# Batch 2's second MLP product as three quads of half-size products

## The chip, the core and the metric

The kernel runs on one core of a Trainium2 chip. Five engines work side by side, each through its own instruction stream in program order: TensorE (PE) for matrix products, with weight loads shown beside it as PEld; VectorE (DVE), ScalarE (ACT) and GpSimd (POOL) for elementwise work; SyncE (SP), which here only issues DMAs. The metric is the device time of one execution in microseconds (us), the lower the better. Before the change it is 298.46 us, the median of three runs from 298.05 to 299.08.

## The reference

Inputs are fp32: q, k, v of shape (4, 8, 768, 64), block numbers, and the weights of an MLP. Per batch, cut to what matters:

```python
scores = np.matmul(q, k.T) / 8.0            # 8 heads, 768 x 768
scores = np.where(mask, scores, -1e9)       # blocks of 32, sampled
x = softmax(scores) @ v                     # heads joined: (768, 512)
a1 = alpha1 * x + beta1
u = x + lam * (w_tok @ a1)                  # token product, 768 x 768
a2 = alpha2 * u + beta2
h = np.maximum(a2 @ w_ch1, 0.0)             # first MLP product, 512 -> 2048
out = u + lam * (h @ w_ch2)                 # second MLP product, 2048 -> 512
```

## The kernel before

A batch has 768 tokens, held as 6 tiles of 128, and 8 heads, done as 4 pairs; there are 16 pairs in all, and pairs 12 to 15 are batch 3's. The attention of batch b + 1 is woven with the MLP of batch b. Everything is issued in an order that is written out by hand: tables of strings (`W1`, `W2`, `W2L`, `W3`), each string a row, each letter a job. A letter whose list of jobs is empty does nothing. Every job issues its instructions to all engines at its place, so a letter's place sets its place in the queues of PE, DVE, ACT, POOL and SP at once.

The letters that matter: `q` computes three units of scores on PE and the first exponential on ACT; `x` does the next exponential; `k` multiplies an exponentiated unit by the mask on DVE (line 636); `p` multiplies weights with v on PE, and when a head is complete DVE divides by the sum (lines 688 and 689, a "finish") and the normalised, scaled values `a1pp` are written by POOL, or by DVE for the last pair (lines 705 and 706); `T` is one third of a token product for two pairs (line 846 on PE, then the sum into `x_sb` at line 858 and two casts at 865 on DVE, or the casts on ACT for the last two pairs); `f` is one step of the first MLP product (four products of 384 columns at line 919 on PE, a rectification at line 926 on ACT into `hts`); `g` is one step of the second MLP product; `S` a sum of parts of `hts` on DVE (line 1144); `W` and `A` sums of weights on DVE; `d` a DMA transpose issued by SP; `a` the DVE `a1pp` of the last pair's first head.

Rows of `W2L` are named r0 to r11 here, from the first. Three rows make a pair of heads. The trace shows the scores of r9 at 225.17, of r10 at 229.66 and of r11 at 235.51 us; r5 to r8 begin at 196.74, 203.54, 211.41 and 218.35. After r11 comes the first row of `W3`, which begins `a p p p g s g g T`: the last masks and products with v, the last finish, and the first `T` of the last head pairs.

The hidden values of a batch are in two tiles `hts`: columns c = 0 for token tiles 0 to 2, c = 1 for 3 to 5. `f` fills c = 0 first. A batch's second MLP product is done in one of two ways. Directly (`job_f2`): a token tile takes 4 steps `g` of four products of 512 columns, all into one bank of PSUM, and one DVE add of 512 columns into `x_sb` (line 1067). Or as a quad (`job_p`): two token tiles together are a 2 x 2 block product, which is done with seven products of blocks instead of eight (1 to 7). Each is one step `g` of eight products of 256 columns (line 1170). Beside them stand four DVE sums for the tile pair (`SOP`; 1 and 2 make X1 and X2, 3 and 4 overwrite parts of `hts`) and seven DVE adds into `x_sb` (line 1180), six of 256 columns and one (product 5) of 512. Products 1, 6 and 5 accumulate in one bank, with a DVE add after each; so do 7 and 4. In batch 2, tiles 0 and 3 are done directly and (1, 4) and (2, 5) as quads; batch 3 is three quads.

PSUM tiles `mm` come from a pool of three banks; `f`, `T`, the first unit of a row's scores (two tiles) and most `g` use it. `sp` has two, `op` (the products with v) one.

Of the kernel before, what the change touches and what calls it, by code (L numbers as in the profile page):

```python
# [18 lines left out]
B = 4  # L19
H = 8  # L20
S = 768
# [4 lines left out]
DM = 512  # L26
P = 128
NT = S // P
# [52 lines left out]
]  # L81
W3 = [
# [6 lines left out]
HN = NH // 2  # L89
# [159 lines left out]
def kernel(  # L249
# [16 lines left out]
    nc = tc.nc  # L266
# [194 lines left out]
    def sp_tile():  # L461
        return psum.tile([P, 2, 512], FP, name="sp", tag="sp", bufs=2)
# [6 lines left out]
    def mm_tile(shape=(P, DM), dt=FP):  # L469
        return psum.tile(list(shape), dt, name="mm", tag="mm", bufs=3)  # L470

    def op_tile(shape):
        phase["op"] += 1
        if phase["first"] and phase["op"] % 2 == 0:
            return mm_tile(shape)
        return psum.tile(shape, FP, name="op", tag="op", bufs=1)
# [97 lines left out]
    x_sbs = {}  # L574
# [234 lines left out]
    did = set()  # L809
# [3 lines left out]
    hts = {}  # L813
# [256 lines left out]
    def emit_store(b, o, sl, eng=nc.sync):  # L1070
        eng.dma_start(
            out[b].rearrange("(p o) n -> p o n", o=NT)[:, o, sl], x_sbs[b][:, o, sl]
        )
# [13 lines left out]
    def b_rows(name, n, k=1):  # L1087
        if name in bq:
            rows, cols = bq[name]
            return w2b[:, rows.start + n : rows.start + n + k, cols]  # L1090
        m = HN * ("T1", "T2", "T4", "T3").index(name) + n
        assert m // 6 == (m + k - 1) // 6
        return tpool[m // 6][:, m % 6 : m % 6 + k]
# [21 lines left out]
    def a_of(b, t, name, r=slice(0, HN)):  # L1115
        if name in ("X1", "X2"):
            return xs[(b, t, name)][:, r]
        c, half = {"11": (0, 0), "12": (0, 1), "21": (1, 0), "22": (1, 1)}[name]
        return hts[(b, c)][:, HN * half + r.start : HN * half + r.stop, ts(t, P)]

    SOP = {
        1: ("X1", "21", "22", ALU.add),
# [5 lines left out]
    def job_s(b, t, n, r=slice(0, HN)):  # L1128
        dst, a, c, op = SOP[n]
        rows = range(r.start, r.stop)  # L1130
        for name in (a, c):
            if name[0] == "X":
                assert all(("S", b, t, int(name[1]), m) in did for m in rows)
            else:
                h, half = divmod(int(name) - 11, 10)
                assert all(("f", b, h, HN * half + m) in did for m in rows)
        if n == 3:
            assert all(("S", b, t, 1, m) in did for m in rows)
        if n == 4:
            assert (b, t, 2) in did  # L1140
        if dst[0] == "X" and (b, t, dst) not in xs:
            tag, bufs = ("eT", 6) if b == B - 1 else ("xs", 4)
            xs[(b, t, dst)] = ap_.tile([P, HN, P], BF, name="xs", tag=tag, bufs=bufs)
        nc.vector.tensor_tensor(
            out=a_of(b, t, dst, r), in0=a_of(b, t, a, r), in1=a_of(b, t, c, r), op=op
        )
        did.update(("S", b, t, n, m) for m in rows)
# [8 lines left out]
        7: ("21", "T3", 3),  # L1156
    }
    banks = {}

    def mul(b, t, n, ps, start, cols=slice(0, HC)):  # L1160
        a, m, need = PROD[n]
        assert m in bq or all((m, r) in did for r in range(0, HN, 2))
        if need:
            assert all(("S", b, t, need, r) in did for r in range(HN))
        c, half = {"1": (0, 0), "X": (1, 0)}.get(a[0], (1, 0))
        if need == 0:
            h, half = divmod(int(a) - 11, 10)
            assert all(("f", b, h, HN * half + r) in did for r in range(HN))
        for r in range(HN):
            nc.tensor.matmul(  # L1170
                ps,
                a_of(b, t, a)[:, r],
                b_rows(m, r)[:, 0, cols],
                start=(start and r == 0),
                stop=(r == HN - 1),
                skip_group_check=True,
            )

    def plus(x, ps):
        nc.vector.tensor_tensor(out=x, in0=x, in1=ps, op=ALU.add)  # L1180

    def twice(ps):
        return ps.unsqueeze(1).broadcast_to([P, 2, HC])

    lo, hi = slice(0, HC), slice(HC, DM)

    def job_p(b, t, n):
        x = x_sbs[b]
        last = (b, t) == (B - 1, NT // 2 - 1)
        bk = banks.setdefault((b, t), {})  # L1190
        if n in (1, 2, 7):
            bk[n] = sp_tile()[:, 0] if n == 1 else mm_tile()[:]
        if n == 3 and not last and 2 not in bk:
            bk[2] = mm_tile()[:]
        if n == 1:
            mul(b, t, 1, bk[1][:, lo], True)
            plus(x[:, t, lo], bk[1][:, lo])
        elif n == 2:
            mul(b, t, 2, bk[2][:, lo], True)
            if last or b < B - 1:  # L1200
                plus(x[:, t, lo], bk.pop(2)[:, lo])
            if last:
                emit_store(b, t, lo)
        elif n == 6:
            mul(b, t, 6, bk[1][:, lo], False)
            plus(x[:, t + 3, lo], bk[1][:, lo])
        elif n == 7:
            mul(b, t, 7, bk[7][:, lo], True)
            plus(x[:, t + 3, hi], bk[7][:, lo])
        elif n == 5:  # L1210
            mul(b, t, 5, bk[1][:, lo], False)
            plus(x[:, t : t + 4 : 3, hi], twice(bk[1][:, lo]))
        elif n == 4:
            mul(b, t, 4, bk[7][:, lo], False)
            plus(x[:, t + 3, lo], bk[7][:, lo])
            emit_store(b, t + 3, slice(0, DM))
        elif last:
            for h in range(2):
                sl = slice(HC + h * P, HC + h * P + P)
                ps = (mm_tile(), op_tile([P, DM]))[h]  # L1220
                mul(b, t, 3, ps[:, sl], True, ts(h, P))
                plus(x[:, t, sl], ps[:, sl])
                emit_store(b, t, sl, (nc.sync, nc.scalar)[h])
        else:
            sl = hi if b < B - 1 else slice(0, DM)
            mul(b, t, 3, bk[2][:, hi], b < B - 1)
            plus(x[:, t, sl], bk[2][:, sl])
            emit_store(b, t, slice(0, DM))
        did.add((b, t, n))

    NPAIR = B * NP
# [34 lines left out]
    def start_mlp(b):  # L1266
        if b == B - 1:
            todo["f"] += [
                lambda j=j: job_m(*j) if len(j) == 2 else job_f1(*j) for j in last_f1()
            ]  # L1270
        else:
            todo["f"] += [
                lambda c=c, n=n: job_f1(b, c, n) for c in range(2) for n in range(NH)
            ]
        if b not in STR:
            todo["g"] += [
                lambda o=o, g=g: job_f2(b, o, g) for o in range(NT) for g in range(4)
            ]
            return
        todo["g"] += [  # L1280
            lambda j=j: job_p(b, *j) if len(j) == 2 else job_f2(b, *j[:2])
            for j in P_ORDER[b]
        ]
        todo["S"] += [lambda t=t, n=n, r=r: job_s(b, t, n, r) for t, n, r in S_ORDER[b]]

    REST = (6, 7, 5, 4, 3)
    P_ORDER = {
        2: [(0, g, "g") for g in range(4)]
        + [(t, 2) for t in (1, 2)]
        + [(3, g, "g") for g in range(4)]  # L1290
        + [(t, 1) for t in (1, 2)]
        + [(t, n) for t in (1, 2) for n in REST],
        3: [(t, n) for t in range(2) for n in (1, 2)]
        + [(t, n) for t in range(2) for n in REST]
        + [(2, n) for n in (1, 2) + REST],
    }
    ALL, R1, R2 = slice(0, HN), slice(0, HN // 2), slice(HN // 2, HN)
    S_ORDER = {
        2: [(t, n, ALL) for t in (1, 2) for n in (1, 2, 3, 4)],
        3: [(t, n, R1) for n in (1, 2, 3) for t in range(3)]  # L1300
        + [(t, n, r) for t in range(3) for n, r in ((1, R2), (2, R2), (3, R2), (4, ALL))],
    }

    def start_pair(i):
# [227 lines left out]
```

## Time and profile before

| | |
|---|---|
| median of three runs | 298.46 us (298.05 to 299.08) |
| profiled execution | 298.76 us |
| its span, first to last instruction | 297.1 us |
| granted TensorE clock | 1.0 |
| PE busy | 289.7 us, 98% |
| DVE busy | 237.8 us, 80% |
| ACT busy | 217.1 us, 73% |
| POOL busy | 109.8 us, 37% |

A row of the time line gives the start and the length in us, the engine, the source line, the operation, the tiles written and read, their shapes and how many instructions were merged. The square bracket at its end is the time for which the engine stood idle before it and what ended that. Instructions overlap at their ends, so what one costs in a queue is read from start to start, not from its length. Records of a few matrix products are missing from a trace now and then.

### The profile page before, as it was taken

The page shows a single profiled execution, that of the slowest core. Times are in us where ns is not written, and L with a number is a line of the kernel's source. Part 1 is how long each engine was busy: PE and PEld are TensorE (multiplying, and loading weights), DVE is VectorE, ACT ScalarE, POOL GpSimd, SP SyncE. Part 2 cuts the span into 40 slices and gives each one's busy share as a digit, 9 for nine tenths or more (in the row PEclk, how much of TensorE's full clock was granted, in tenths as well). Part 3 has the DMA queues.
Part 4 walks back from the last instruction along what each step waited for, and adds up shares of the span by engine and source line. Part 5 has one row for each costly group of instructions (what it writes and reads, how often), then busy time and mean ns, then how long its engine had stood idle before and what let it go on. Part 6 is the DMA issues. An engine that isn't in the chain of part 4 may idle for free.

```text
span 297.1 us, 7554 instructions
## 1 busy us (share of the span) xinstructions
PE 289.7 (98%) x3082; PEld 193.5 (65%) x3101; DVE 237.8 (80%) x485; ACT 217.1 (73%) x324; POOL 109.8 (37%) x149
## 2 busy tenths in 40 slices
PE   8999999999999999999999999999999999999995
PEld 3688888665567565565576466556576679665884
DVE  4988899995678796977878777895956899799774
ACT  4999999998899963999779581999869744576000
POOL 8997978632443710355323340335320300000000
PEclk9999999999999999999999999999999999999999
DMA  6999999992392995729955767745520211400032
GB/s 182 184 199 186 192 171 187 171 123 44 95 147 55 112 203 84 118 65 119 125 96 73 124 110 146 103 92 69 70 62 17 38 38 29 141 1 3 0 141 73
DMA packets 57274, 31.09 MB, mean 105 GB/s; under 512 B 37204, under 2 KB 54016, under 8 KB 57240
## 3 DMA queue, kind: packets, MB, share of 16 engines
q0 software_dynamic: 16752, 14.22, 34.4%
q1 hardware_dynamic: 40020, 15.92, 29.3%
q8 instruction: 24, 0.39, 0.6%
q10 hardware_dynamic: 468, 0.47, 0.5%
q14 instruction: 10, 0.08, 0.1%
HBM read 29.75 MB, written 6.29 MB: 121 GB/s over the span
## 4 chain that ended last, share of the span: by engine, by line
PE 84%; DVE 6%; DMA 4%; ACT 3%; issue 1%; POOL 1%; SPq 0%; POOLq 0%
PE mm L919 18%; PE mm L1058 13%; PE sp L601 10%; PE mm L846 8%; PE op L671 7%; PE mm L1170 5%; PE sp L1170 4%; PE mm L601 3%; DVE eT L636 3%; PE mm L822 3%; PE op L648 2%; DMA vr<-in_v_dram 2%; ACT eT L619 2%; PE mm L1016 2%; PE sp L1016 2%; DMA uraw<-ubf 2%
## 5 line engine op out<-in xcount | busy, mean ns | idle before, releaser
L619 ACT ACTIVATE eT<-sp,expb 128x1024 f16<-128x1024 f32 x111 | 118.4, 1120 | 2.1 <-PE sp L601 1.4
L636 DVE TENSOR_TENSOR eT<-eT,mask 128x1024 f16<-128x1024 f16 x99 | 80.6, 843 | 13.5 <-ACT eT L619 13.3
L919 PE MATMUL mm<-uT,w1b 128*128 128x384 bf16 x416 | 76.8, 326 | 0.4 <-ACT hts L926 0.3
L705 POOL TENSOR_TENSOR a1pp<-x_sb,vbc 128x384 bf16<-128x384 f32 x25 | 28.5, 1138 | 119.0 <-DVE x_sb L689 84.7
L619 ACT ACTIVATE eT<-mm,expb 128x512 f16<-128x512 f32 x66 | 41.7, 685 | 26.5 <-PE mm L601 26.3
L926 ACT ACTIVATE hts<-mm 128x384 bf16<-128x384 f32 x104 | 49.1, 502 | 13.3 <-PE mm L919 12.4
L919 PEld LDWEIGHTS <-w1b 128*128 128x128 bf16 x416 | 38.7, 98 | 26.4 <-issue 2.9
L1058 PE MATMUL mm<-w2b,hts 128*128 128x512 bf16 x205 | 52.2, 379 | 0.9 <-issue 0.2
L671 PEld LDWEIGHTS <-eT 128*128 128x128 f16 x792 | 29.8, 98 | 8.8 <-issue 1.7
L1058 PEld LDWEIGHTS <-hts 128*128 128x128 bf16 x224 | 19.8, 98 | 22.3 <-issue 3.9
L671 PE MATMUL op<-vext,eT 128*128 128x65 f16 x792 | 32.1, 194 | 0.4 <-DVE x_sb L689 0.3
L601 PE MATMUL sp<-qTs,kTs 88*128 88x512 bf16 (+1 forms) x120 | 26.9, 325 | 1.2 <-ACT eT L619 0.7
L706 POOL TENSOR_TENSOR a1pp<-a1pp,vbc 128x384 bf16<-128x384 bf16 x25 | 26.7, 1069 | 2.0
L846 PE MATMUL mm<-a1pp,wtokT 128*128 128x256 bf16 x216 | 25.9, 273 | 0.1
L846 PEld LDWEIGHTS <-wtokT 128*128 128x128 bf16 x216 | 20.6, 98 | 5.6 <-issue 1.8
L1170 PEld LDWEIGHTS <-hts 128*128 128x128 bf16 x208 | 19.5, 98 | 3.0 <-issue 0.3
L858 DVE TENSOR_TENSOR x_sb<-x_sb,mm 128x512 f32<-128x512 f32 x18 | 12.3, 686 | 9.9 <-PE mm L846 9.8
L601 PE MATMUL sp<-qhT,khT 64*128 64x256 bf16 (+1 forms) x176 | 19.8, 322 | 0.0
L601 PEld LDWEIGHTS <-khT 64*128 64x128 bf16 x264 | 10.6, 94 | 12.7 <-issue 9.2
L648 PEld LDWEIGHTS <-eT 128*128 128x128 f16 x360 | 14.9, 97 | 3.8 <-issue 0.3
L689 DVE TENSOR_TENSOR x_sb<-op,rcp 128x384 f32<-128x384 f32 x28 | 15.6, 558 | 1.0
L1067 DVE TENSOR_TENSOR x_sb<-x_sb,mm 128x512 f32<-128x512 f32 x14 | 9.6, 686 | 8.2 <-PE mm L1058 6.7
(135 smaller groups left out, 376.9 us busy)
## 6 DMA issues: line engine op xcount, KB each, us to landing
out_dram<-x_sb SPq DMA_DIRECT2D x23, 256.0 KB
qpad<-in_q_dram POOLq DMA_DIRECT2D x15, 192.0 KB, 4.6
kr<-in_k_dram POOLq DMA_DIRECT2D x15, 192.0 KB, 5.3
vr<-in_v_dram POOLq DMA_DIRECT2D x15, 192.0 KB, 6.3
w1b<-in_moe_w_ch_dram POOLq DMA_DIRECT2D x4, 512.0 KB, 9.2
w2b<-in_moe_w_ch_dram POOLq DMA_DIRECT2D x4, 512.0 KB, 7.7
hts<-in_moe_w_tok_dram POOLq DMA_DIRECT2D x2, 576.0 KB, 8.7
x_sb<-in_k_dram ACTq DMA_DIRECT2D x2, 192.0 KB
```

The source lines that it names most:

```text
L601: nc.tensor.matmul(sp[jj][:, dst], lhsT, rhs, start=True, stop=True, skip_group_check=True,)
L619: nc.scalar.activation(dst, at, AF.Exp, bias=expb[:], scale=SCALE)
L636: nc.vector.tensor_mul(out=e, in0=e, in1=keep)
L648: nc.tensor.matmul(op[0][:, o, :], ets[u][:, jj, h * QB + n * P : h * QB + n * P + P], vexts[i % NVB][:, w, 2 * jp + jj, :], start=op[1] == 0,
L671: nc.tensor.matmul(op[0][:, o, :], ets[u][:, jj, h * QB + n * P : h * QB + n * P + P], vexts[i % NVB][:, w, 2 * jp + jj, :], start=op[1] == 0,
L705: eng.tensor_tensor(out=dst, in0=x_sbs[b][:, :, cols], in1=bc[0], op=ALU.mult)
L706: eng.tensor_tensor(out=dst, in0=dst, in1=bc[1], op=ALU.add)
L846: nc.tensor.matmul(ps[:, o], wtokT[:, os_, ts(2 * n + o, P)], a1pps[i][:, os_, :], start=(os_ == 0 and o == 0), stop=(os_ == NT - 1 and o ...
L919: nc.tensor.matmul(ps[:, 0:QC], w1b[:, dk, ts(n, P)], uTs[b][:, dk, ts(c, QC)], start=(dk == 0), stop=(dk == 3),)
L926: nc.scalar.activation(h_row(b, c, n), ps[:, 0:QC], AF.Relu)
L1058: nc.tensor.matmul(ps[:], ht[:, nk, ts(o % 3, P)], w2b[:, nk, :], start=(nk == 0), stop=(nk == NH - 1),)
L1170: nc.tensor.matmul(ps, a_of(b, t, a)[:, r], b_rows(m, r)[:, 0, cols], start=(start and r == 0), stop=(r == HN - 1), skip_group_check=True,)
```

## The change

Batch 2's second MLP product becomes three quads: tiles (0, 1), (2, 5) and (3, 4). Tiles 0 and 1 both lie in c = 0, so the first quad needs only the first 16 steps `f`. A quad is now named by its pair of tiles instead of by its lower tile. In `W2L`, `f` steps move from r8 to r10 into r6 and r7, the four direct steps of r6 and r7 and the four of r10 and r11 go, five of the eight `W` move from r6 to r5, and four `S` are added. The first quad's order is 2, 1, 6, 5, 7, 3, 4: product 2 at the end of r8; 1, 6 and 5 in r9, where `T` moves behind 1 and 6; 7, 3 and 4 in r10. Its first bank is an `mm` tile, where other quads of the batch take an `sp` tile, and product 3 gets a tile of its own. `W3` is not changed: 11 steps `g` of batch 2 are left to it, as before, now of quads (2, 5) and (3, 4).

```diff
@@ -71,13 +71,13 @@
     "q g 0 k g d 1 2 p x k g x k",
     "q 0 p k x v Q v 1 2 p k x g k g",
     "q 0 p 1 g x k f K k x f p p k 2 f",
-    "q k 0 f x f p s f f x 1 L p k 2 f f f k Y f",
-    "q f L f 0 f k W W W W W W W W 1 f Y x f p g x f p f g k k 2",
-    "q x k x k Q 0 g 1 s f f g p 2 p f f k p f",
-    "q T 0 k f 1 x k f T x f 2 p k K p f",
-    "q x 0 x T k 1 k f 2 k f Q f d p L",
-    "q x 0 x K k g d k s f g f 1 k p p S S g 2",
-    "q p Y x x k g k S 0 1 k 2 g v g v g",
+    "q k 0 f x f p s f f x 1 L p k W W 2 f f f k Y W W W f",
+    "q f L f 0 f k W W W 1 f f S Y x f p f x f p f f k k 2",
+    "q x f k x f k Q 0 1 s f f p 2 p f f k S p f",
+    "q T 0 k f 1 x k f T x f 2 p k K p g",
+    "q S S g x 0 x f g T k g 1 k 2 k Q d p L",
+    "q x g 0 x K k d g k s 1 k p p g S S 2",
+    "q p Y x x k g k S 0 1 k 2 g v g v",
 ]
 W3 = [
     "a p p p g s g g T S T S T S S S d g g U g v g D g D D g D g D g D D",
@@ -1115,8 +1115,14 @@
     def a_of(b, t, name, r=slice(0, HN)):
         if name in ("X1", "X2"):
             return xs[(b, t, name)][:, r]
-        c, half = {"11": (0, 0), "12": (0, 1), "21": (1, 0), "22": (1, 1)}[name]
-        return hts[(b, c)][:, HN * half + r.start : HN * half + r.stop, ts(t, P)]
+        o, half = t[int(name[0]) - 1], int(name[1]) - 1
+        return hts[(b, o // 3)][:, HN * half + r.start : HN * half + r.stop, ts(o % 3, P)]
+
+    def a_ready(b, t, name, rows):
+        if name[0] == "X":
+            return all(("S", b, t, int(name[1]), m) in did for m in rows)
+        o, half = t[int(name[0]) - 1], int(name[1]) - 1
+        return all(("f", b, o // 3, HN * half + m) in did for m in rows)
 
     SOP = {
         1: ("X1", "21", "22", ALU.add),
@@ -1128,12 +1134,7 @@
     def job_s(b, t, n, r=slice(0, HN)):
         dst, a, c, op = SOP[n]
         rows = range(r.start, r.stop)
-        for name in (a, c):
-            if name[0] == "X":
-                assert all(("S", b, t, int(name[1]), m) in did for m in rows)
-            else:
-                h, half = divmod(int(name) - 11, 10)
-                assert all(("f", b, h, HN * half + m) in did for m in rows)
+        assert a_ready(b, t, a, rows) and a_ready(b, t, c, rows)
         if n == 3:
             assert all(("S", b, t, 1, m) in did for m in rows)
         if n == 4:
@@ -1156,16 +1157,14 @@
         7: ("21", "T3", 3),
     }
     banks = {}
+    LATE = [(2, (2, 5)), (2, (3, 4))] + [(3, (o, o + 3)) for o in range(3)]
 
     def mul(b, t, n, ps, start, cols=slice(0, HC)):
         a, m, need = PROD[n]
         assert m in bq or all((m, r) in did for r in range(0, HN, 2))
         if need:
             assert all(("S", b, t, need, r) in did for r in range(HN))
-        c, half = {"1": (0, 0), "X": (1, 0)}.get(a[0], (1, 0))
-        if need == 0:
-            h, half = divmod(int(a) - 11, 10)
-            assert all(("f", b, h, HN * half + r) in did for r in range(HN))
+        assert a_ready(b, t, a, range(HN))
         for r in range(HN):
             nc.tensor.matmul(
                 ps,
@@ -1185,47 +1184,50 @@
     lo, hi = slice(0, HC), slice(HC, DM)
 
     def job_p(b, t, n):
-        x = x_sbs[b]
-        last = (b, t) == (B - 1, NT // 2 - 1)
+        x, (o1, o2) = x_sbs[b], t
+        tail = b == B - 1
+        last = tail and o2 == NT - 1
         bk = banks.setdefault((b, t), {})
-        if n in (1, 2, 7):
-            bk[n] = sp_tile()[:, 0] if n == 1 else mm_tile()[:]
-        if n == 3 and not last and 2 not in bk:
-            bk[2] = mm_tile()[:]
+        if n == 1 and (b, t) in LATE:
+            bk[1] = sp_tile()[:, 0]
+        elif n in (1, 2, 7) or (n == 3 and not tail):
+            bk[n] = mm_tile()[:]
         if n == 1:
             mul(b, t, 1, bk[1][:, lo], True)
-            plus(x[:, t, lo], bk[1][:, lo])
+            plus(x[:, o1, lo], bk[1][:, lo])
         elif n == 2:
             mul(b, t, 2, bk[2][:, lo], True)
-            if last or b < B - 1:
-                plus(x[:, t, lo], bk.pop(2)[:, lo])
+            if last or not tail:
+                plus(x[:, o1, lo], bk[2][:, lo])
             if last:
-                emit_store(b, t, lo)
+                emit_store(b, o1, lo)
         elif n == 6:
             mul(b, t, 6, bk[1][:, lo], False)
-            plus(x[:, t + 3, lo], bk[1][:, lo])
+            plus(x[:, o2, lo], bk[1][:, lo])
         elif n == 7:
             mul(b, t, 7, bk[7][:, lo], True)
-            plus(x[:, t + 3, hi], bk[7][:, lo])
+            plus(x[:, o2, hi], bk[7][:, lo])
         elif n == 5:
             mul(b, t, 5, bk[1][:, lo], False)
-            plus(x[:, t : t + 4 : 3, hi], twice(bk[1][:, lo]))
+            plus(x[:, o1 : o2 + 1 : o2 - o1, hi], twice(bk[1][:, lo]))
         elif n == 4:
+            assert {(b, t, m) for m in (5, 6, 7)} <= did
             mul(b, t, 4, bk[7][:, lo], False)
-            plus(x[:, t + 3, lo], bk[7][:, lo])
-            emit_store(b, t + 3, slice(0, DM))
+            plus(x[:, o2, lo], bk[7][:, lo])
+            emit_store(b, o2, slice(0, DM))
         elif last:
             for h in range(2):
                 sl = slice(HC + h * P, HC + h * P + P)
                 ps = (mm_tile(), op_tile([P, DM]))[h]
                 mul(b, t, 3, ps[:, sl], True, ts(h, P))
-                plus(x[:, t, sl], ps[:, sl])
-                emit_store(b, t, sl, (nc.sync, nc.scalar)[h])
+                plus(x[:, o1, sl], ps[:, sl])
+                emit_store(b, o1, sl, (nc.sync, nc.scalar)[h])
         else:
-            sl = hi if b < B - 1 else slice(0, DM)
-            mul(b, t, 3, bk[2][:, hi], b < B - 1)
-            plus(x[:, t, sl], bk[2][:, sl])
-            emit_store(b, t, slice(0, DM))
+            assert {(b, t, m) for m in (1, 2, 5)} <= did
+            sl, ps = (slice(0, DM), bk[2]) if tail else (hi, bk[3])
+            mul(b, t, 3, ps[:, hi], not tail)
+            plus(x[:, o1, sl], ps[:, sl])
+            emit_store(b, o1, slice(0, DM))
         did.add((b, t, n))
 
     NPAIR = B * NP
@@ -1283,22 +1285,33 @@
         ]
         todo["S"] += [lambda t=t, n=n, r=r: job_s(b, t, n, r) for t, n, r in S_ORDER[b]]
 
+    def direct(*tiles):
+        return [(o, g, "g") for o in tiles for g in range(4)]
+
+    def quad(t, order):
+        return [(t, n) for n in order]
+
     REST = (6, 7, 5, 4, 3)
     P_ORDER = {
-        2: [(0, g, "g") for g in range(4)]
-        + [(t, 2) for t in (1, 2)]
-        + [(3, g, "g") for g in range(4)]
-        + [(t, 1) for t in (1, 2)]
-        + [(t, n) for t in (1, 2) for n in REST],
-        3: [(t, n) for t in range(2) for n in (1, 2)]
-        + [(t, n) for t in range(2) for n in REST]
-        + [(2, n) for n in (1, 2) + REST],
+        2: quad((0, 1), (2, 1, 6, 5, 7, 3, 4))
+        + quad((2, 5), (2,))
+        + quad((3, 4), (2,))
+        + quad((2, 5), (1,))
+        + quad((3, 4), (1,))
+        + quad((2, 5), REST)
+        + quad((3, 4), REST),
+        3: quad((0, 3), (1, 2))
+        + quad((1, 4), (1, 2))
+        + quad((0, 3), REST)
+        + quad((1, 4), REST)
+        + quad((2, 5), (1, 2) + REST),
     }
     ALL, R1, R2 = slice(0, HN), slice(0, HN // 2), slice(HN // 2, HN)
+    Q3 = [(0, 3), (1, 4), (2, 5)]
     S_ORDER = {
-        2: [(t, n, ALL) for t in (1, 2) for n in (1, 2, 3, 4)],
-        3: [(t, n, R1) for n in (1, 2, 3) for t in range(3)]
-        + [(t, n, r) for t in range(3) for n, r in ((1, R2), (2, R2), (3, R2), (4, ALL))],
+        2: [(t, n, ALL) for t in ((0, 1), (2, 5), (3, 4)) for n in (1, 2, 3, 4)],
+        3: [(t, n, R1) for n in (1, 2, 3) for t in Q3]
+        + [(t, n, r) for t in Q3 for n, r in ((1, R2), (2, R2), (3, R2), (4, ALL))],
     }
 
     def start_pair(i):
```

## The prediction

> **What bounds the kernel now.** Read first: the page's busy shares and the shares of its chain.
>
> ```profile
> PE 289.7 (98%) x3082; PEld 193.5 (65%) x3101; DVE 237.8 (80%) x485; ACT 217.1 (73%) x324; POOL 109.8 (37%) x149
> PE 84%; DVE 6%; DMA 4%; ACT 3%; issue 1%; POOL 1%; SPq 0%; POOLq 0%
> ```
>
> TensorE (PE) is the bound over the whole span. The change, however, touches only rows r5 to r11 of `W2L`, so the second view is the busy time of each engine in the stretches of r5, r6, r7, r9, r10, and of r11 with the start of `W3`. Its columns: from:to, length, then busy time (instructions) of PE, of PE's weight loads, DVE, ACT and POOL, the granted clock, and DMA.
>
> ```profile
> 196.70:203.50 6.80, 6.80 (x65) 4.09 (x64) 5.28 (x9) 6.54 (x12) 3.89 (x4) 1.00 0.27 69
> 203.50:211.40 7.90, 7.85 (x68) 4.48 (x68) 5.70 (x13) 6.76 (x12) 1.58 (x3) 1.00 1.03 129
> 211.40:218.30 6.90, 6.85 (x72) 4.06 (x72) 5.44 (x8) 5.02 (x8) 2.47 (x2) 1.00 0.21 57
> 225.10:229.60 4.50, 4.50 (x45) 3.07 (x44) 2.24 (x6) 4.33 (x8) 0.00 (x0) 1.00 0.01 4
> 229.60:235.50 5.90, 5.73 (x63) 3.86 (x60) 5.65 (x10) 4.62 (x8) 2.24 (x2) 1.00 0.35 67
> 235.50:244.10 8.60, 8.52 (x102) 6.04 (x102) 7.91 (x17) 5.10 (x6) 0.00 (x0) 1.00 0.09 32
> ```
>
> In r9 VectorE (DVE) works 2.24 of 4.50 us; in the next two stretches it works 5.65 of 5.90 and 7.91 of 8.60, beside a PE that is as full. Which of them binds there is told by the third view, the chain of waits near the first token product of the last head pairs (L846, 244.07):
>
> ```profile
> 236.84 0.21 DVE rcp L688
> ...
> 243.46 0.57 DVE a1pp L706
> 244.03 0.05 issue
> 244.07 0.28 PE mm L846
> ```
>
> For the last 7 us before that product the chain runs on DVE. I call its start the gate: all that is left of the kernel follows it, and the same work stands behind it before and after the change. So the question is when the gate opens.
>
> **The change part by part.** First PE. Its rows around r9 and around the products:
>
> ```profile
> 225.92 1.48 PE L846 MATMUL mm<-a1pp,wtokT 128*128 128x256 bf16 x12
> 227.24 2.11 PE L919 MATMUL mm<-uT,w1b 128*128 128x384 bf16 x12
> 229.19 0.53 PE L671 MATMUL op<-vext,eT 128*128 128x65 f16 x12
> ...
> 236.65 2.75 PE L1058 MATMUL mm<-w2b,hts 128*128 128x512 bf16 x12
> 239.23 1.04 PE L1170 MATMUL sp<-w2b,hts 128*128 128x256 bf16 x8
> 240.11 1.27 PE L671 MATMUL op<-vext,eT 128*128 128x65 f16 x36
> ```
>
> From start to start twelve full-size products take 239.23 - 236.65 = 2.58 us, 0.215 each, and eight half-size ones 240.11 - 239.23 = 0.88, 0.110 each. The two direct tiles are 8 steps of four (0.86 a step), the new quad is 7 steps of eight (0.88 a step): 32 x 0.215 = 6.88 us becomes 56 x 0.110 = 6.16. PE is spared 0.7 us. A half-size product brings a weight load of its own (98 ns below), still shorter than 110 ns, so it stays hidden.
>
> ```profile
> L1170 PEld LDWEIGHTS <-hts 128*128 128x128 bf16 x208 | 19.5, 98 | 3.0 <-issue 0.3
> L926 ACT ACTIVATE hts<-mm 128x384 bf16<-128x384 f32 x104 | 49.1, 502 | 13.3 <-PE mm L919 12.4 <-DVE uT L989 0.2
> ```
>
> The Trainium skill speaks against this. TensorE: Matmul & The Clock Gate, section Back-to-back issue gap, gives a sustained roofline of about 131 ns a product at 512 columns and about 81 ns at 128, which puts 32 full-size products at 4.2 us and 56 half-size ones at no less than 4.5, a loss of at least 0.3 us. The trace does not agree with it (215 and 110 ns).
>
> The earlier `f` steps: three more in r6 and two more in r7, each with a rectification of 0.50 us on ScalarE (ACT). ACT works 6.76 + 5.02 = 11.78 of 14.80 us there; five more make 14.3. PE alone would need less: five `f` of 0.65 (227.24 to 229.19 holds three) for four direct steps of 0.86, so 3.25 for 3.44, 0.2 less. ACT is then nearly full and PE waits for its PSUM tiles now and then. I bound the shift of r8's start by -0.4 (PE alone, its present small gaps gone too) and +0.3 (ACT at its limit), and take 0, between them. The eight weight sums `W`, five of which move into r5, find 6.80 - 5.28 = 1.5 us free on DVE there and relieve r6 by as much as they cost r5; without that cover r5 would be longer by at most their excess of a microsecond. I cost this, and the sums X1 and X2 of the new quad in r6 and r7 (DVE free for 2.2 and 1.5 us), at nothing.
>
> Now DVE from r8's end to the gate:
>
> ```profile
> 227.44 0.69 DVE L858 TENSOR_TENSOR x_sb<-x_sb,mm 128x512 f32<-128x512 f32 x1 [2.22 <-PE mm L846]
> 228.17 0.49 DVE L865 CAST ubf<-x_sb 128x256 bf16<-128x256 f32 x2
> 228.58 1.89 DVE L636 TENSOR_TENSOR eT<-eT,mask 128x1024 f16<-128x1024 f16 x3
> 230.38 0.19 DVE L688 RECIPROCAL rcp<-op 128x6 f32<-128x6 f32 x1
> 230.61 0.56 DVE L689 TENSOR_TENSOR x_sb<-op,rcp 128x384 f32<-128x384 f32 x1
> 231.38 1.41 DVE L636 TENSOR_TENSOR eT<-eT,mask 128x1024 f16<-128x1024 f16 x1 [0.21 <-ACT eT L619]
> 232.71 0.41 DVE L1180 TENSOR_TENSOR x_sb<-x_sb,mm 128x256 f32<-128x256 f32 x1
> 233.04 1.07 DVE L636 TENSOR_TENSOR eT<-eT,mask 128x1024 f16<-128x1024 f16 x1
> ...
> 234.97 0.68 DVE L1144 TENSOR_TENSOR xs<-hts 128x1024 bf16<-128x1024 bf16 x1
> 235.68 0.69 DVE L1144 TENSOR_TENSOR xs<-xs,hts 128x1024 bf16<-128x1024 bf16 x1
> 236.84 0.20 DVE L688 RECIPROCAL rcp<-op 128x6 f32<-128x6 f32 x1 [0.47 <-PE op L671]
> ...
> 240.06 0.68 DVE L1067 TENSOR_TENSOR x_sb<-x_sb,mm 128x512 f32<-128x512 f32 x1
> 240.66 0.41 DVE L1180 TENSOR_TENSOR x_sb<-x_sb,sp 128x256 f32<-128x256 f32 x1
> ```
>
> (1) The token product T in r9 is issued right behind the scores now. Afterwards there stand ahead of it quad product 1, an `f` and product 6: 0.88 + 0.65 + 0.88 = 2.41 us, and r8 ends in product 2 (0.88) where it ended in an `f` (0.65): 0.23 more. PE stays in order, so T's sum on DVE (227.44) comes 2.6 us later, at about 230.1. The three mask multiplications of r9 (228.58), which the softmax of the last pair needs, are queued behind that sum on DVE, and all of r10 and r11 behind them. Meanwhile DVE has the two sums S3 and S4 and the adds of products 2, 1 and 6 (2 x 0.71 and 3 x 0.33, 2.4 us): it fits into the 2.22 us for which DVE waits at present plus the 2.6 us, and DVE still idles about 2.4 us (2.22 + 2.6 - 2.4). That time is lost to it.
>
> (2) From T's sum to the gate DVE took 244.03 - 227.44 = 16.6 us, with 0.21 and 0.47 us of waits. Afterwards: the same nine masks, three finishes, two a1pp pairs and three S sums (two in r10, one in r11, for other tiles). The adds differ. Before: one of 512 columns (0.60 to the next start, 240.06 to 240.66) and three of 256 (0.33, 232.71 to 233.04), 1.6 us. Afterwards: product 5 (512 columns, 0.60), products 7, 3 and 4, and the three openings of the other quads (six of 0.33), 2.6 us. That is 1.0 us more. With all of DVE 2.6 us late, ACT's exponentials and PE's products are done before DVE asks for them, so its waits of 0.7 go. The run becomes 16.6 + 1.0 - 0.7 = 16.9 us.
>
> (3) The masks at 231.38 and 233.04 took 1.41 and 1.07 us while GpSimd (POOL) wrote the normalised values:
>
> ```profile
> 231.24 1.00 POOL L705 TENSOR_TENSOR a1pp<-x_sb,vbc 128x384 bf16<-128x384 f32 x1 [10.51 <-DVE x_sb L689]
> ```
>
> The pair moves along with the finish of r9, so this tax of 1.1 us (1.33 + 0.99 from start to start, less 2 x 0.60) stays. Its ends are 0, if it falls on PSUM adds alone (the one at 232.71 took no more than its 0.41), and 1.5.
>
> Sum: the gate goes from 244.07 to 230.1 + 16.9 = 247.0, 2.9 us later. PE's saved 0.7 us is inside it and buys nothing, since PE then waits at the gate. The stores and the two DMA transposes move on SP's queue with their adds; both transposes stay ahead of the quad's first store, and nothing waits for them before the gate. The profiled execution took 298.76 us (span 297.1 and 1.7 around it), 0.3 above the median of 298.46: 301.7 against the first, **301.4 us** against the median. Its own range: with r8 at -0.4 and the tax 0, 299.9; with r8 at +0.3, the tax at 1.5 and half of the waits staying, 302.4.
>
> **The rivals.** A difference under 0.3% (0.9 us) can't be told from none.
> - DVE keeps up and PE remains the bound. For: PE is 98% busy, and 8.52 of 8.60 us in the stretch that ends at the gate. Place and price: DVE's run from T's sum would have to end by 243.3, which is 13.2 us after 230.1; the rows give 16.9. It decides if DVE can win 3.7 us there, for instance if masks are issued ahead of T's sum. Time: 298.46 - 0.7, and 0.2 more if r6 and r7 lose their small gaps: 297.6, on the edge of what can be told. Chance 0.14.
> - T's delay is hidden: DVE's masks are late, but the run has more slack than two waits show. Then only the extra adds count, +1.0 - 0.7: 298.8. Chance 0.08.
> - ACT binds r6 and r7 by more than I allow: three rectifications of r6 that have to pass ahead of r7's scores cost up to 1.5 us, on top of 2.9: 302.9. Against: exponentials can wait behind two free score tiles. Chance 0.06.
> - The half-size products pay their weight loads: 56 x 0.098 = 5.5 us on PE. Against: 110 ns from start to start over an existing chain. Time 303 to 306. Chance 0.01. The roofline that the Trainium skill gives in TensorE: Matmul & The Clock Gate, Back-to-back issue gap, would be a small form of this.
> - The change not doing what it says: the chain 1, 6, 5 opens and closes inside r9, and 7, 4 inside r10, so no scores are issued while one is open on PE. But the add of product 5 is behind T's sum and one mask on DVE, so product 7, which takes the same bank, waits for it half a microsecond on PE. That lies beside DVE's run and costs nothing.
>
> **How the numbers follow.** The forecast holds 0.71. Range 299.0 to 302.7: it takes in the forecast's own and part of the second and third rival. Faster by over 0.3%: 0.09, most of the first rival. Within 0.3%: 0.12, the rest of it and most of the second. Slower: 0.79.
>
> **What would show it.** Right: the third T sum of r9 stands some 2.5 us further behind r9's scores on DVE; DVE waits twice in r9 and then hardly at all up to the gate; PE has idle stretches in r10, r11 and ahead of the gate, several tenths each, released by DVE; and the end moves as far as the gate does. Wrong: PE without gaps up to the gate, or a gate later for another reason (ACT ahead of r7's scores). The forecast fails if DVE's operations can be reached in another order than I read from the row's letters, or if its run from T's sum to the gate takes under 14 us.

## The result

The changed kernel takes 301.20 us (median of five, 301.10 to 301.49) where the kernel before takes 298.58 (five, 298.05 to 299.08). The ratio is 1.0085, with a 95% interval from 1.0073 to 1.0097: slower, by 2.6 us, which is clear of the noise though small. The forecast was 301.4.

The page of the changed kernel, engines and chain:

```profile
PE 290.4 (97%) x3125; PEld 195.7 (65%) x3125; DVE 242.4 (81%) x494; ACT 216.8 (72%) x324; POOL 109.8 (37%) x149
PE 90%; DVE 6%; ACT 2%; DMA 1%; issue 0%; ACTq 0%
```

By this page nothing has happened: the shares are those of before, and the chain is even more of PE. The stretch must be cut out. From the first scores of r8 to the gate (the first token product of the last head pairs), in the kernel before:

```profile
218.35:244.07 25.72, 25.47 (x276) 17.81 (x276) 20.06 (x40) 18.96 (x28) 4.16 (x4) 1.00 0.13 30
```

and in the changed kernel:

```profile
218.06:246.43 28.37, 25.84 (x297) 19.92 (x297) 23.23 (x48) 16.93 (x23) 4.16 (x4) 1.00 0.13 34
```

(Columns: from:to, length, busy time of PE, weight loads, DVE, ACT and POOL, clock, DMA.) The stretch is 2.65 us longer. DVE works 3.2 us more in it. PE was busy all but 0.25 us of it and now stands still for 2.5 us. This length, from r8's scores to the gate, is the measure for all that follows; behind the gate both kernels take 53.0 us to the end of the span (297.1 - 244.07 and 299.4 - 246.43).

The time line of DVE in the changed kernel, from the end of r8 into r10:

```profile
225.21 0.42 DVE L1179 TENSOR_TENSOR x_sb<-x_sb,mm 128x256 f32<-128x256 f32 x1 [0.28 <-PE mm L1169]
225.55 0.68 DVE L1145 TENSOR_TENSOR hts<-hts 128x1024 bf16<-128x1024 bf16 x1
226.15 0.69 DVE L1145 TENSOR_TENSOR hts<-hts,xs 128x1024 bf16<-128x1024 bf16 x1
226.95 0.42 DVE L1179 TENSOR_TENSOR x_sb<-x_sb,mm 128x256 f32<-128x256 f32 x1
228.49 0.42 DVE L1179 TENSOR_TENSOR x_sb<-x_sb,mm 128x256 f32<-128x256 f32 x1 [1.12 <-PE mm L1169]
229.80 0.69 DVE L858 TENSOR_TENSOR x_sb<-x_sb,mm 128x512 f32<-128x512 f32 x1 [0.89 <-PE mm L846]
230.53 0.50 DVE L865 CAST ubf<-x_sb 128x256 bf16<-128x256 f32 x2
230.94 0.68 DVE L636 TENSOR_TENSOR eT<-eT,mask 128x1024 f16<-128x1024 f16 x1
231.54 0.68 DVE L1179 TENSOR_TENSOR x_sb<-x_sb,mm 128x512 f32<-128x512 f32 x1
232.14 1.28 DVE L636 TENSOR_TENSOR eT<-eT,mask 128x1024 f16<-128x1024 f16 x2
...
234.36 1.38 DVE L636 TENSOR_TENSOR eT<-eT,mask 128x1024 f16<-128x1024 f16 x1
235.67 0.41 DVE L1179 TENSOR_TENSOR x_sb<-x_sb,mm 128x256 f32<-128x256 f32 x1
236.00 1.68 DVE L636 TENSOR_TENSOR eT<-eT,mask 128x1024 f16<-128x1024 f16 x2
```

The first row is the add of product 2, the next two are S3 and S4. DVE then waits 1.12 and 0.89 us for PE, for product 6 and for T, and the first mask of r9 (L636, 230.94) stands behind T's sum (229.80). After it DVE has no wait until the gate. The chain of waits there:

```profile
228.46 1.32 PE mm L846 x12
229.78 0.02 issue
229.80 0.70 DVE x_sb L858
...
245.82 0.57 DVE a1pp L706
246.38 0.05 issue
```

It goes from PE to DVE at T's sum and stays on DVE for 16.6 us. Before, it lay on DVE for only the last 7. PE's side of the same, rows with a wait ahead of them:

```profile
232.10 0.82 PE L1169 MATMUL mm<-qk,hts 128*128 128x256 bf16 x6 [0.34 <-ACT eT L619]
...
238.06 1.91 PE L1169 MATMUL mm<-w2b,hts 128*128 128x256 bf16 x16 [0.51 <-DVE x_sb L1179]
...
242.83 0.54 PE L671 MATMUL op<-vext,eT 128*128 128x65 f16 x12 [0.66 <-DVE eT L636]
...
246.43 3.78 PE L846 MATMUL mm<-a1pp,wtokT 128*128 128x256 bf16 x33 [0.44 <-DVE a1pp L706]
```

The first wait, that of product 7, ends with an exponential of ACT. After it PE waits for adds, masks and a1pp of DVE, up to the gate itself.

### The profile page after: what moved, and what is told of

It reads as the page before. It is cut to its first block, busy times and chain, and to the rows that moved or that the text cites. A ratio compares the mean times of both kernels' runs of the same rounds, so it can differ in the third digit from the quotient of the medians.

```text
span 299.4 us, 7630 instructions
## 1 busy us (share of the span) xinstructions
PE 290.4 (97%) x3125; PEld 195.7 (65%) x3125; DVE 242.4 (81%) x494; ACT 216.8 (72%) x324; POOL 109.8 (37%) x149
## 4 chain that ended last, share of the span: by engine, by line
PE 90%; DVE 6%; ACT 2%; DMA 1%; issue 0%; ACTq 0%
PE mm L919 22%; PE mm L1058 14%; PE sp L601 11%; PE mm L846 8%; PE op L671 8%; PE mm L1169 6%; PE sp L1169 4%; PE mm L601 3%; PE mm L822 3%; PE op L648 2%; DVE eT L636 2%; PE mm L1016 2%; PE sp L1016 2%; PE mm L648 1%; ACT eT L619 1%; DMA ms<-ms_c 1%
## 5 line engine op out<-in xcount | busy, mean ns | idle before, releaser
L636 DVE TENSOR_TENSOR eT<-eT,mask 128x1024 f16<-128x1024 f16 x99 | 79.8, 834 | 11.1 <-ACT eT L619 11.0
L1058 PE MATMUL mm<-w2b,hts 128*128 128x512 bf16 x192 | 46.8, 380 | 0.0
L1058 PEld LDWEIGHTS <-hts 128*128 128x128 bf16 x192 | 16.9, 98 | 19.4 <-issue 3.6
L1169 PEld LDWEIGHTS <-hts 128*128 128x128 bf16 x248 | 23.3, 98 | 4.3 <-issue 1.6
L601 PE MATMUL sp<-qhT,khT 64*128 64x512 bf16 (+1 forms) x176 | 20.0, 322 | 0.0
L858 DVE TENSOR_TENSOR x_sb<-x_sb,mm 128x512 f32<-128x512 f32 x18 | 12.3, 685 | 8.5 <-PE mm L846 8.5
L1067 DVE TENSOR_TENSOR x_sb<-x_sb,mm 128x512 f32<-128x512 f32 x12 | 8.2, 685 | 8.2 <-PE mm L1058 8.2
```

The lines of the kernel that those rows point to most:

```text
L601: nc.tensor.matmul(sp[jj][:, dst], lhsT, rhs, start=True, stop=True, skip_group_check=True,)
L636: nc.vector.tensor_mul(out=e, in0=e, in1=keep)
L1058: nc.tensor.matmul(ps[:], ht[:, nk, ts(o % 3, P)], w2b[:, nk, :], start=(nk == 0), stop=(nk == NH - 1),)
L1169: nc.tensor.matmul(ps, a_of(b, t, a)[:, r], b_rows(m, r)[:, 0, cols], start=(start and r == 0), stop=(r == HN - 1), skip_group_check=True,)
```

## The experiments

The theory: T's sum comes late on DVE, the masks are queued behind it, and DVE's run from there sets the gate. The rivals: PE sets the gate, by its amount or by its order; or DVE's added work does it and not the order. Beside each measured time stands the ratio to the kernel before from the same chip, with its interval. The changed kernel's is 1.0085 (1.0073 to 1.0097).

### The masks ahead of T

```diff
-    "q S S g x 0 x f g T k g 1 k 2 k Q d p L",
+    "q S S g x 0 x f k g k k T g 1 2 Q d p L",
```

Only DVE's order changes.

> Changed kernel with the three masks of r9 issued ahead of T, so that DVE multiplies them while it waits for PE; PE's and ACT's order is untouched. If the loss is the queue behind T's sum on DVE, the masks fill the waits of 1.12 and 0.89 us, T's sum starts at most 0.2 us later, and the gate opens 1.2 to 1.6 us earlier: about 299.8 us. If the loss is that T itself comes late on PE, or PE's own gaps, nothing moves: 301.2.

299.93 us, ratio 1.0051 (1.0034 to 1.0068). The stretch:

```profile
218.39:245.18 26.79, 25.14 (x297) 19.77 (x297) 22.73 (x48) 16.93 (x23) 4.16 (x4) 1.00 0.13 35
```

28.37 has become 26.79, 1.58 us less, with PE's and ACT's instructions in the same order as in the changed kernel. On DVE the masks now run while it used to wait, and T's sum follows them without a wait:

```profile
229.16 1.28 DVE L636 TENSOR_TENSOR eT<-eT,mask 128x1024 f16<-128x1024 f16 x2
230.36 0.68 DVE L858 TENSOR_TENSOR x_sb<-x_sb,mm 128x512 f32<-128x512 f32 x1
```

So more than half of the 2.65 us was the place of three masks in DVE's queue. The other 1.07 us remains. In time the gain is smaller: from 1.0085 to 1.0051 is 1.0 us, and the two intervals don't meet. (A stretch is read from one execution of a kernel, a ratio from several, so the two need not agree to some tenths.)

### T late in the kernel before

```diff
-    "q x 0 x T k 1 k f 2 k f Q f d p L",
+    "q x 0 x f f f T k 1 k 2 k Q d p L",
```

> Kernel before, with T of r9 put behind the row's three f steps (1.95 us of PE); no work added or taken away, no quad. If DVE's run from T's sum sets the gate, T's sum comes 1.95 us later, the run loses its 0.7 us of waits, and the end moves by +1.2: about 299.8 us. If PE sets the gate, the order of PE's work does not matter: 298.5.

300.74 us, ratio 1.0080 (1.0065 to 1.0095): as slow as the changed kernel, without a quad and without any work added. Here T was later than meant. Its own row on PE, and its sum on DVE:

```profile
229.01 1.47 PE L846 MATMUL mm<-a1pp,wtokT 128*128 128x256 bf16 x12 [1.31 <-ACT hts L926]
```

```profile
230.51 0.69 DVE L858 TENSOR_TENSOR x_sb<-x_sb,mm 128x512 f32<-128x512 f32 x1 [5.64 <-PE mm L846]
```

Behind three `f`, T's bank was still held by a rectification that ACT does after the row's exponentials (1.31 us). The sum started 230.51 - 218.00 = 12.51 us after r8's scores where it was 9.09 before (227.44 - 218.35): 3.4 later, not 1.95. The gate moved by 2.2 (stretch 27.93). The direction and the mechanism hold, and 1.2 of the 3.4 us were caught up, more than the 0.7 that I had put down for DVE's waits.

### Three adds left out

In r10, products 7, 3 and 4 of the first quad without their DVE adds.

> Changed kernel without the three DVE adds of products 7, 3 and 4 of the first quad in r10 (tiles 0 and 1 of batch 2 lack these terms). If DVE's run sets the gate, it shortens by 3 x 0.33: about 300.2 us. If PE sets it: 301.2.

300.93 us, ratio 1.0086 (1.0067 to 1.0105); in time this can't be told from the changed kernel, and the 300.2 that was expected did not come. In its profile the stretch is 27.82, 0.55 less. One row on DVE shows where the other half went:

```profile
234.28 3.41 DVE L636 TENSOR_TENSOR eT<-eT,mask 128x1024 f16<-128x1024 f16 x3
```

Three masks take 3.33 us to the next start (237.61) where three at 0.60 would take 1.8, while POOL writes a1pp from 234.44 on. With the adds between them the masks paid 1.1 us for POOL's company in the changed kernel (234.36 to 235.67 and 236.00 to 237.60, less 3 x 0.60), without them 1.5. An add from PSUM beside POOL took no more than elsewhere (0.41), so it had been a cheap filling.

### PE's work taken away

In r10, one matrix product instead of eight in each of the steps 7, 3 and 4.

> Changed kernel with one matrix product instead of eight in each of the steps 7, 3 and 4 of the first quad in r10 (tiles 0 and 1 of batch 2 lack these terms): 21 x 0.109 = 2.3 us less on PE, DVE as it was. If DVE's run sets the gate, PE only waits longer: 301.2 us, at most 0.3 less. If PE sets it: 298.9.

The stretch:

```profile
219.00:247.37 28.37, 24.73 (x276) 18.50 (x276) 23.24 (x48) 16.93 (x23) 4.15 (x4) 0.94 0.13 34
```

To the hundredth as long as in the changed kernel, with 21 products fewer. DVE's run from T's sum (230.74) to the end of the last a1pp (247.31) has no wait and takes 16.6 us, as in the changed kernel. So PE's amount of work does not set the gate, which is what the run was for. PE's busy time fell by 1.1 us (25.84 to 24.73) and not by the 2.3 of the products, since its clock was lower here, 0.94; the last section comes back to that. The time was 301.84 us, ratio 1.0114 (1.0097 to 1.0131), 0.6 longer than expected, and that is not explained. In the profile the excess is there ahead of r5 already (its scores start at 197.13 against 196.19), where no step was changed and where the profiled executions of all these kernels lie between 196.07 and 197.87.

### T's place on PE

Two kernels: T straight behind r9's scores, and T in r8.

```diff
-    "q S S g x 0 x f g T k g 1 k 2 k Q d p L",
+    "q S S T x 0 x k g f k g k p g 1 2 Q d L",
```

> Changed kernel with T of r9 right behind the row's scores again, ahead of products 1, 6 and 5 and of the f step, the masks behind T's sum. If T's lateness is what makes DVE late, T's sum starts at about 227.4 instead of 229.8 (with r8's scores at 218.06), the finish of r9 ends 1 to 1.5 us earlier and the gate opens as much earlier: about 300.0 us. If the new work of the quad on DVE makes the loss, it stays at 301.2 less 0.3.

300.71 us, ratio 1.0072 (1.0057 to 1.0087).

```diff
-    "q T 0 k f 1 x k f T x f 2 p k K p g",
-    "q S S g x 0 x f g T k g 1 k 2 k Q d p L",
+    "q T 0 k f 1 x k f T x f 2 p T k K p g",
+    "q S S g x 0 x f k g k g 1 k 2 Q d p L",
```

> Changed kernel with the third T moved from r9 into r8, between that row's two products with v, where DVE waits for PE now. T's sum leaves r9 altogether. By DVE's queue: r9 holds 5.3 us of DVE work, the gate opens some 2.2 us earlier than in the changed kernel and 0.5 later than before: about 299.2 us. If PE's order is what counts, r9's scores are 1.3 us later and the gain is under 1 us: 300.4 or more.

300.89 us, ratio 1.0075 (1.0060 to 1.0090). Both miss the earlier gate that T's place was to bring: by these intervals neither can be told from the changed kernel, and the stretches are 27.66 and 27.89. An earlier T alone is not worth what I expected. With T first, PE meets a wait of another kind, and with T in r8 it meets it twice:

```profile
230.01 0.60 PE L1169 MATMUL mm<-qTs,xs 128*128 128x256 bf16 x4 [0.72 <-DVE x_sb L1179]
```

```profile
227.68 1.03 PE L1169 MATMUL mm<-w2b,hts 128*128 128x256 bf16 x8 [0.24 <-DVE x_sb L1179]
...
230.77 1.03 PE L1169 MATMUL mm<-qTs,xs 128*128 128x256 bf16 x8 [0.51 <-DVE x_sb L1179]
```

Products 1, 6 and 5 share a bank, and each of the later two has to wait for the add of the one before. T had been a good filling between 6 and 5. Without it the scores of r10 come at 232.52 and 232.10 us, 14.0 and 13.8 after r8's; in the changed kernel they come 12.9 after (230.94 - 218.06). Scores that come later bring later exponentials and masks.

### The quad's work spread out

Three kernels, all with every operation of the change. In the first, T is in r8, product 2 in r7, S3 and S4 in r8, and X1 and X2 of the next quad in r9. The second has products 7, 3 and 4 in r9 besides. The third has product 2 in r7, S3 and S4 in r8, and T behind r9's scores:

```diff
-    "q x f k x f k Q 0 1 s f f p 2 p f f k S p f",
-    "q T 0 k f 1 x k f T x f 2 p k K p g",
-    "q S S g x 0 x f g T k g 1 k 2 k Q d p L",
+    "q x f k x f k Q 0 1 s f f p 2 p f f k S p g",
+    "q S S T 0 k f 1 x k f T x f 2 p k K p f",
+    "q x 0 x k T g f k g p k g 1 2 Q d L",
```

> As e6_T_in_r8, and product 2 at the end of r7, the last two f steps in r8, S3 and S4 at the start of r8, X1 and X2 of the next quad at the start of r9 instead of in r10. No work is added or left out. 2.5 us of DVE work leave r9 and r10 for r8, where DVE idles. By DVE's queue the gate comes as early as before the change, less 0.1 to plus 0.4: 298.5 to 299.0 us. If DVE's run does not set the gate: as e6_T_in_r8.

> As e7_spread, and products 7, 3 and 4 of the first quad moved from r10 into r9, 7 between 1 and 6, so that r10 has two products and r11 one. DVE's work from r10 to the gate falls to 9.9 us. By DVE's queue the gate comes up to 0.6 us earlier than before the change, and the 0.7 us saved on PE show: about 298.0 us. If r9 becomes too full for PE or DVE, as e7_spread or up to 0.6 later.

> Changed kernel, no work added or left out: product 2 at the end of r7 and the f step that stood there at the end of r8, S3 and S4 at the start of r8 where DVE idles, and T of r9 right behind the scores with one mask ahead of it. Nothing is put ahead of r9's or r10's scores. Two things set the gate by now: DVE's queue and the time of the last pair's scores. Both are served here: T's sum 2.4 us earlier, 1.2 us of sums gone from r9. Gate about as before the change: 298.4 to 299.2 us. If one of the two is wrong, no better than the kernel with the masks ahead of T: 299.9.

300.63 (ratio 1.0058, 1.0041 to 1.0075), 300.81 (1.0073, 1.0058 to 1.0088) and 300.60 us (1.0065, 1.0044 to 1.0086): all three miss the first figure of their expectation by 1.4 us or more, and the less good outcome that each names as its second came instead. None is better than the masks ahead of T. The stretches are 27.34, 27.68 and 27.24. The time line of DVE in the third shows why:

```profile
227.28 0.69 DVE L636 TENSOR_TENSOR eT<-eT,mask 128x1024 f16<-128x1024 f16 x1 [1.81 <-ACT eT L619]
...
230.55 0.42 DVE L1179 TENSOR_TENSOR x_sb<-x_sb,mm 128x256 f32<-128x256 f32 x1 [0.52 <-PE mm L1169]
...
234.28 0.42 DVE L1179 TENSOR_TENSOR x_sb<-x_sb,mm 128x256 f32<-128x256 f32 x1 [1.38 <-PE mm L1169]
```

DVE work taken out of r9 leaves waits of 1.81 us for the first exponential and 1.38 for product 7 in its place. A row's masks can't fill DVE before the row's scores have been through ACT.

### Product 4 behind the last scores

```diff
-    "q x g 0 x K k d g k s 1 k p p g S S 2",
-    "q p Y x x k g k S 0 1 k 2 g v g v",
+    "q x g 0 x K k d g k s 1 k p p S S 2",
+    "q p Y x x k g k g S 0 1 k 2 g v g v",
```

> As e9_T_and_sums_early, and product 4 moved behind r11's scores, which come 0.88 us earlier. If the last scores set the gate, 0.3 to 0.8 us earlier than e9_T_and_sums_early; if DVE's queue alone sets it, no difference.

> As e2_masks_first, and product 4 behind r11's scores (0.88 us earlier). In e2_masks_first DVE has no wait from r11 to the gate: if its queue sets the gate there, 299.9 as in e2_masks_first; if the scores set it, about 299.2.

300.48 us (ratio 1.0062, 1.0041 to 1.0082) beside 300.60, and 300.05 (1.0047, 1.0028 to 1.0065) beside 299.93. No difference in either pair, and the stretches agree to 0.02 us (27.22 with 27.24; for the second, this row beside 26.79):

```profile
218.72:245.51 26.79, 25.22 (x297) 20.06 (x297) 22.72 (x48) 16.93 (x23) 4.16 (x4) 1.00 0.13 35
```

Here r11's scores came 0.9 us earlier (235.12 - 218.72 = 16.40 against 235.67 - 218.39 = 17.28) and the gate did not. In all four kernels DVE waits for product 7 in r10, 0.4 us in one pair and 1.4 in the other, and then has no wait up to the gate: from there on its queue sets the time.

### No work of the quad on DVE

As with the masks ahead of T, and without S3, S4 and the seven adds of the first quad. X1 and X2, in r6 and r7, stay.

> As e2_masks_first, and without S3, S4 and the seven DVE adds of the first quad (tiles 0 and 1 of batch 2 get no second MLP product): all of PE's work stays, 3.8 us of DVE work between r8 and the gate goes. If what e2_masks_first still loses is DVE's amount of work, the gate opens earlier than before the change and PE's saved 0.7 us show: 297.8 to 298.3 us. If it is the order of PE (scores and exponentials of the last pair), it stays above 299.

298.95 us, ratio 1.0017 (1.0007 to 1.0027): between the two times that were expected. The stretch, and the first masks of r9 and of r10 on its DVE:

```profile
218.66:244.37 25.71, 24.89 (x297) 19.65 (x297) 19.16 (x39) 16.93 (x23) 4.15 (x4) 1.00 0.14 37
```

```profile
227.43 0.69 DVE L636 TENSOR_TENSOR eT<-eT,mask 128x1024 f16<-128x1024 f16 x1 [1.89 <-ACT eT L619]
...
233.24 0.79 DVE L636 TENSOR_TENSOR eT<-eT,mask 128x1024 f16<-128x1024 f16 x1 [0.83 <-ACT eT L619]
```

25.71 us, that of the kernel before, though nine DVE operations of the quad are gone. The 1.07 us that the masks ahead of T had left over goes with DVE's work for the quad (in time 1.0 us, from 1.0051 to 1.0017). And what PE saves does not show even when that work costs nothing: DVE then waits for exponentials. Those of r10 wait for scores that stand behind the quad's products in r9 and come 12.85 us after r8's (231.51 - 218.66), where before the change it was 11.31 (229.66 - 218.35). Of the 0.5 us that are left in time, half lies ahead of r8: from r5's scores to r8's it is 21.87 us here (196.79 to 218.66) and 21.61 before the change. No kernel tried here beats the one before.

## Why the prediction was right

Its steps, from r8's scores where places are compared, since the two executions differ by 0.55 us ahead of r5 already. The starts of r5 and r8 in the kernel before, then in the changed one:

```profile
196.74 0.39 PE L601 MATMUL mm<-qhT,khT 64*128 64x256 bf16 x4
...
218.35 0.39 PE L601 MATMUL mm<-qhT,khT 64*128 64x256 bf16 x4
```

```profile
196.19 0.39 PE L601 MATMUL mm<-qhT,khT 64*128 64x256 bf16 x4
...
211.09 0.56 PE L601 MATMUL mm<-qhT,khT 64*128 64x512 bf16 x2
...
218.06 0.39 PE L601 MATMUL mm<-qhT,khT 64*128 64x256 bf16 x4
```

- **The products and what PE saves.** Right: PE's amount did not matter (21 products fewer, same stretch), and the weight loads did not show: in the changed kernel's trace eight half-size products took 0.87 us (229.60 to 230.47) and, in an earlier batch, eight full-size ones 1.73 (110.87 to 112.60), 109 and 216 ns each. The low roofline for full-size products, which the Trainium skill gives in TensorE: Matmul & The Clock Gate, section Back-to-back issue gap, would have made them the cheaper kind; the trace disagreed before the change and disagrees after it.
- **r8's shift.** Taken as 0, bounded at -0.4 and +0.3. From r5's scores to r8's it is 21.61 us before and 21.87 afterwards: +0.26, near the upper bound. r6 is 0.23 longer (202.99 to 211.09, against 203.54 to 211.41), which is what three `f` cost in place of two direct steps (1.95 for 1.72). r7 should then have been shorter by about 0.4, with two `f` in place of two direct steps (1.30 for 1.72), and was not: 6.97 us against 6.94. What took these 0.4 us is not shown. The first scores of r7 (0.56 instead of 0.39) are one place of it, and ACT, which was to be nearly full there, is a likely cause.
- **T's lateness.** Predicted 2.6 us, measured from r8's scores 11.74 - 9.09 = 2.65. DVE's lost time was put at 2.4 and is 2.3: 0.28 ahead of product 2's add, 1.12 and 0.89.
- **DVE's run from T's sum to the gate.** Predicted 16.9, measured 246.38 - 229.80 = 16.6, as long as before. The added 1.0 us of adds and POOL's tax of 1.1 are there. What was sized wrong is the waits that go. I took the 0.68 us that the brackets give. From start to start the two cost 0.85: the mask at 231.38 began 0.77 after the multiplication at 230.61 where 0.48 is usual, and the finish at 236.84 began 1.16 after the sum at 235.68 where 0.60 is. A further 0.1 went at two masks of r11, which took 1.30 (237.55 to 238.85) where 1.20 is usual, a gap too small for a bracket. With these 0.95 us the run comes to 16.6.
- **The gate.** Predicted 2.9 us later. From r5's scores it is 2.65 + 0.26 = 2.91. That this meets the forecast so closely is luck, two errors of 0.3 that cancel. The medians differ by 2.6, and the median of before, from which the forecast was counted, has moved from 298.46 to 298.58 with two more runs.
- **The rivals.** PE as the bound fell with the run that took PE's work away. Its condition, masks ahead of T's sum, was then tried, and DVE won 1.58 us by it, not 3.7. T's delay was not hidden: DVE caught up its own small waits and no more. Of ACT's price in r6 and r7, up to 1.5 us, at most the 0.4 of r7 exist. Product 7 did wait in r10, 0.34 us, beside DVE's run, but not for the add of product 5: the trace has an exponential of ACT as what ended the wait, and product 7 began at 232.10, before that add (231.54, 0.68 long) was over.

What I did not see is how little a better order could win. The forecast blamed T's lateness. The experiments split the 2.65 us into 1.58 for the masks behind T's sum, which a line of the table wins back, and then 1.07 for DVE's work on the quad, which none of my orders won back (in time, 1.0 us each); and T's place on PE by itself, in two kernels, gave nothing that can be told in time. My later expectations, for the spread-out kernels, added up DVE's work and forgot that the row's exponentials have to be there first. When they are there is set by PE's order: by the place of the row's scores, and by products of one bank that wait for each other's adds ahead of them.

## To carry to other kernels

A saving on the busiest engine is worth what the stretch it lies in is bound by; cut the stretch out between two marks that both kernels have, and compare lengths there, since the page's shares stayed the same through a loss of 2.6 us. Where an order is written by hand, an operation that waits for another engine must not stand ahead of operations that are ready: moving three ready masks ahead of one waiting sum was worth 1.6 us of the stretch and 1.0 us of the time. A block product with one multiplication fewer pays in sums and adds on another engine, here 4.6 us more of DVE (242.4 us busy for 237.8) for 0.7 of PE, and is for stretches in which that engine idles.

## What the runs showed of the hardware

Two things that I had not expected.

When PE's work was taken away in r10, the granted clock fell to half for about 3.4 us (the third column from the end is the mean clock of each 2 us; at half clock it stands for 0.6, 2.0 and 0.8 us):

```profile
234.00:236.00 2.00, 0.89 (x20) 0.89 (x21) 1.97 (x5) 1.57 (x2) 0.86 (x1) 0.85 0.51 99
236.00:238.00 2.00, 1.90 (x17) 0.87 (x14) 2.00 (x4) 0.50 (x1) 1.38 (x2) 0.50 0.06 23
238.00:240.00 2.00, 2.00 (x25) 1.48 (x23) 1.97 (x5) 2.00 (x4) 0.00 (x0) 0.80 0.42 153
```

It follows a wait of 1.64 us on PE, in the row

```profile
235.11 1.31 PE L671 MATMUL op<-vext,eT 128*128 128x65 f16 x24 [1.64 <-DVE x_sb L689]
```

and did not move the gate, since that was DVE's. The mean clock of the whole execution was 0.992 to 0.994 in all four runs of this kernel and 0.998 or more in every other run, so it is not the accident of one execution. The Trainium skill, TensorE: Matmul & The Clock Gate, section HAM oscillation, warns of idle gaps above some 3.4 us; here one of 1.64, with two single products between it and a shorter wait of 0.34, was followed by half the clock. In the changed kernel's stretch, with waits up to 0.66, the clock stayed at 1.0.

And POOL's tax depends on what stands beside it: three masks in a row paid 1.5 us, the same three with adds from PSUM between them 1.1. That agrees with the Trainium skill, GPSIMD Engine Reference, section Key points, by which POOL shares its SBUF interfaces with VectorE and contends with instructions that have two SBUF inputs: a mask has two, an add of a product one.
